# Two token units of 128 in place of one of 256 in an attention and feed-forward kernel

## The chip, the cores and the metric

The kernel runs on one core of a Trainium2 chip. The metric is the device time of one execution in microseconds (us), the median of several runs. The core has five engines that run beside each other and wait for each other through semaphores: TensorE (PE, matrix products; its weight loads are listed as PEld), VectorE (DVE), ScalarE (ACT), GpSimd (POOL) and SyncE (SP), which here issues nearly all transfers (DMA).

## The reference

Two layers run one after the other. The first is attention that keeps the 32 largest scores of each row; the second is a feed-forward layer with h - tanh(h) between its two matrices.

```python
# q, k, v: (8 batches, 8 heads, 576 tokens, 64), float32
scores = (q @ k^T) / sqrt(64)
kth    = the 32nd largest score of each row
scores = where(scores >= kth, scores, -1e9)
attn   = exp(scores - rowmax); attn = attn / (sum(attn) + 1e-9)
x      = attn @ v                  # reshaped to 4608 tokens x 512
h      = x @ w_in                  # 512 x 2048
g      = h - tanh(h)
out    = g @ w_out                 # 2048 x 512 -> 4608 x 512, float32
```

## The kernel before

**Attention in steps.** `plan()` writes a list of 144 steps. A step handles 128 rows of scores for a pair of heads (`hp`). A batch has 576 = 4 x 128 + 64 tokens: 16 steps for the four blocks of 128, and two more "rem" steps, one for every second head pair, for the last 64 tokens of the batch. So a batch has 18 steps, and half a batch nine. In each turn of the main loop, step n+1 gets its scores (`scores`, L352 on PE, copied by ACT in L360), step n is searched for its largest values on DVE (`search`, L382 to L405), step n-1 is masked and exponentiated (L438, L441, L461 on ACT and POOL), and step n-2 is divided (L487) and transposed (`turn_z`, L519). The transposed rows go through DRAM (`there`, then `spare`, L532 and L535, issued on SP), and a few steps later `values` (L583) multiplies them with v and writes tokens into a unit's `xT` or `xTr` (L603). In batch 0 the transposes are done on PE instead; in batches 1 and 2 the k and q rows are transposed on PE (L312), in the others on DVE (L319). In `scores` the pool of PSUM tiles has one buffer, so that scores of the next step cannot start before DVE has read those of the present one (L390 is its last reader).

**Feed-forward in units.** A `Unit` collects tokens: two blocks of 128 (n = 256), or one (n = 128) for the first two blocks of batch 0. The last 64 tokens of each batch are gathered over four batches into a "rest" unit of 256 with the tag `xTr`: one for batches 0 to 3, one for batches 4 to 7. The tag's pool has one buffer.

When a unit's tokens are complete, `ffn(u)` appends its items to the list `work`. Every item is eight matmul instructions; the profile shows two records for each. For a plain unit of 256 these are:

- 16 hidden items (`ffn_h`): the products with `w_in`, in column halves of 64 (`by_columns`, L627). Every second item ends with tanh and a copy on ACT (L653, L654) and a subtraction on POOL (L655), which leave g.
- 14 output items (`ffn_p`, `product`): the second matrix is applied in a form of Strassen's scheme with seven block products in place of eight. `ORDER` lists them. They need sums of blocks of g (`sum_up`, L829 on POOL), sums of blocks of `w_out` that are made once (`combine`), of which some are fetched again from DRAM for each unit (`bring`, 512 KB a time, on SP), and joins of partial results on POOL (L878).

One corner of `w_out` is changed in place by `combine("T1", ...)`: the block b12 holds b12 - b11 after it. Units of 128 (both in batch 0) use 128-column weights with 128 moving columns (L641) for their hidden items, and come before that change, so that their output items use `w_out` as it was loaded. The first unit of 256, also of batch 0, does the same with 16 output items (`plain`). The last unit of batch 7 and the rest unit of batches 4 to 7 are the tail and use `ffn_s`, which applies the seven products to `w_in` as well.

**What sets the order.** The items are dealt between the parts of the attention steps, first in, first out, by `deal`. The share of a step comes from `rate()`:

```python
have, low, high = len(work), 0.0, None
coming = sorted((t, u.items) for u, t in ready.items() if t > n)
for t, k in coming + [(NS + LAG, 0)]:
    r = have / max(t - n, 1)
    high = r if high is None else min(high, r)
    have += k
...
return max(low, high)
```

`ready` holds the step at which each unit's tokens will be complete, `u.items` the number of its items. The share is thus the largest even rate at which the list does not run dry before the next arrivals; `low` raises it where a buffer is needed again. DVE gets no item in the middle of the kernel, so the order of DVE's instructions does not depend on the shares.

Of the kernel before, what the change touches and what calls it, by code (L numbers as in the profile page):

```python
# [9 lines left out]
ALU = mybir.AluOpType  # L10
FP32 = mybir.dt.float32
# [8 lines left out]
J = 4  # L20
# [36 lines left out]
def kernel(  # L57
# [9 lines left out]
    nc = tc.nc  # L67
    P = nc.NUM_PARTITIONS
    B, H, S, D = q.shape
    DM, DFF = moe_w_in.shape  # L70
    NHP = H // 2
    JP = J * P
    R = S - JP
# [4 lines left out]
    CD = DM // P  # L78
# [5 lines left out]
    WJ = 4  # L84
    FJ = CF // WJ
# [6 lines left out]
    def pool(name, bufs, **kw):  # L92
        return ctx.enter_context(tc.tile_pool(name=name, bufs=bufs, **kw))
# [10 lines left out]
    thpool = pool("th", 4)  # L104
# [7 lines left out]
    bank = [0]  # L112

    def h_bank(k, name):
        return h_ps.tile([P, 512], FP32, tag=f"h{k}", name=name)

    def next_h(name):
        bank[0] ^= 1
        return h_bank(bank[0], name)
# [6 lines left out]
    w_out = [consts.tile([P, FJ, DM], FP32, name=f"w_out{j}") for j in range(WJ)]  # L126
# [91 lines left out]
    def half(t):  # L218
        return slice(t * D, (t + 1) * D)
# [118 lines left out]
    rest = consts.tile([P, 2, S4 + Q], FP32, name="rest")  # L338
# [230 lines left out]
    def values(n):  # L569
# [41 lines left out]
        if n in done:  # L611
            work.extend(ffn(u))
# [9 lines left out]
    cur = {}  # L622

    def by_columns(acc, lhs, rhs, start, stop):

        for t in range(2):
            nc.tensor.matmul(  # L627
                acc[half(t)], lhs[:, half(t)], rhs, start=start, stop=stop, skip_group_check=True
            )
# [45 lines left out]

    def corners(x):
        x = x.rearrange("p (m r) n -> p m r n", r=2)
        return [[x[:, :, r, c * 2 * P : (c + 1) * 2 * P] for c in range(2)] for r in range(2)]  # L680

    def keep_corner(j):

        nc.sync.dma_start(kept_B12[:, 2 * j : 2 * j + 2, :], corners(w_out[j][:])[0][1])

    def bring_corners():

        for j in range(WJ):
            nc.sync.dma_start(corners(w_out[j][:])[0][1], kept_B12[:, 2 * j : 2 * j + 2, :])

    def combine(x, j):

        (b11, b12), (b21, b22) = corners(w_out[j][:])
        k, ms = j // 2, slice(2 * (j % 2), 2 * (j % 2) + 2)
        t2 = whole["T2"][k][:, ms, :]
        if x == "T3":
            nc.gpsimd.tensor_tensor(whole["T3"][k][:, ms, :], b12, b22, ALU.subtract)
        elif x == "T1":
            nc.gpsimd.tensor_tensor(b12, b12, b11, ALU.subtract)
        elif x == "T2":  # L700
            nc.gpsimd.tensor_tensor(t2, b11, whole["T3"][k][:, ms, :], ALU.subtract)
            if k == 0:
                outgoing.append((called[0], lambda: nc.sync.dma_start(kept["T2"][:, ms, :], t2)))
        else:
            t4 = temps[j % 2] if k else whole["T4"][k][:, ms, :]
            nc.gpsimd.tensor_tensor(t4, b21, t2, ALU.subtract)
            if k:
                outgoing.append((called[0], lambda: nc.sync.dma_start(kept["T4"][:, ms, :], t4)))
# [242 lines left out]
    def ffn_small_o(u, part):  # L951

        ffn_o(u, 0, part)
        if u.combines:
            combine_next()

    def ffn_plain_o(u, item):

        ffn_o(u, item // (CF // 2), item % (CF // 2))
        if item % 2:  # L960
            combine_next()
# [13 lines left out]
    def ffn(u):  # L975

        nh = CF * u.n // (2 * P)
        full = len(u.blocks) == 2
        if u.tail:
            nh = 0  # L980
            for item in range(2 * len(ORDER)):
                yield CD * WJ, u, lambda item=item: ffn_s(u, item)
        for item in range(nh):
            f = (item + 1) * CF // nh - 1
            yield CD * (f // FJ + 1), u, lambda item=item: (ffn_full if full else ffn_h)(u, item)
        if not full:
            for part in range(CF // 2):
                yield CD * (WJ + part // 2 + 1), None, lambda part=part: ffn_small_o(u, part)
            return
        if u.plain:  # L990
            for item in range(CF):
                yield 2 * WJ * CD, None, lambda item=item: ffn_plain_o(u, item)
            return
        for item in range(2 * len(ORDER)):
            yield 2 * WJ * CD, None, lambda item=item: ffn_p(u, item)
# [3 lines left out]
    steps, done, work = [], {}, []  # L999

    def plan():
        steps.clear(), done.clear()

        def block(b, qt):
            return [(slice(0, P), out[b * S + qt * P : b * S + (qt + 1) * P, :])]

        rest = None
        for b in range(B):
            if b % 4 == 0:
                rest = Unit(  # L1010
                    [
                        [(half(i), out[(b + k + i) * S + JP : (b + k + i + 1) * S, :]) for i in range(2)]
                        for k in (0, 2)
                    ],
                    "xTr",
                )

            parts = [(0, 1), (2, 3)]
            if b == 0:
                parts[0:1] = [(0,), (1,)]  # L1020
            for a, qts in enumerate(parts):
                unit = Unit([block(b, qt) for qt in qts], "xT")
                unit.tail = b == B - 1 and a == len(parts) - 1
                if unit.tail:
                    rest.tail = True
                    unit.items = rest.items = 4 * len(ORDER)
                pe = b == 0
                unit.combines = pe and a == 1
                unit.plain = pe and a == len(parts) - 1
                if unit.plain:  # L1030
                    unit.items = 32
                for hp in range(NHP):
                    for i, qt in enumerate(qts):
                        steps.append(Step(b, hp, qt, unit, 0, i, len(qts), pe, a))
                    if hp == NHP - 1:
                        done[len(steps) - 1] = unit
                    if hp % 2 and a == (0 if b == B - 1 else len(parts) - 1):
                        steps.append(Step(b, hp - 1, J, rest, b % 4 * R, pe=pe, part=a))
                        if hp == NHP - 1 and b % 4 == 3:
                            done[len(steps) - 1] = rest  # L1040
        for g, after in zip(steps, steps[1:]):
            if after.pe and not after.rem and not g.pe:
                g.lag = 3
# [3 lines left out]

    def run(exact):
        plan()
        turned_pe[0] = not exact  # L1050
        combined[0] = 0
# [237 lines left out]
```

## Time and profile before

| | |
|---|---|
| Median of 3 runs | 1467.79 us (1467.73 to 1472.83) |
| The profiled execution | 1468.51 us |
| Its span (first to last instruction) | 1466.6 us |
| Mean granted TensorE clock | 0.970 of full speed |
| PE busy | 1366.4 us (93%), 13220 records |
| DVE busy | 1321.3 us (90%) |
| POOL busy | 1078.7 us (74%) |
| ACT busy | 1032.7 us (70%) |
| DMA | 240.83 MB, mean 164 GB/s |

The profile is of one execution. Its time is a little longer than its span, which leaves out what lies before the first and after the last instruction. "Busy" is the time in which at least one instruction of an engine runs; matmuls are pipelined and overlap, so a mean duration of one is longer than what a further one costs, and a busy PE is not PE at its peak. In a row of a group of instructions, the numbers after the bar are busy us, mean ns of one, and idle time of the engine just before them with the releasers. In a row of a wait they are us in total, how many times, and the longest.

### The profile page before, as it was taken

To read this page: it belongs to the slowest core of one execution; us is meant where nothing else is said; L and a number is where in the kernel's file an instruction comes from. 1 tells how busy PE (TensorE), PEld (TensorE's weight loads), DVE (VectorE), ACT (ScalarE), POOL (GpSimd) and SP (SyncE) were. 2 spreads that over 40 slices of the span, in tenths; PEclk is the share of its full clock that TensorE was granted. 3 is DMA by queue.
4 is the path that set the end of the run, shared out by engine and by line. 5 is a ranking of instruction groups with operands and counts; after the bars stand their busy time and mean duration, and the time that the engine had idled before them with its cause. 6 is when DMAs were issued, how large, how long until landed. Compare 5 with 4: busy or idle time off the path is not lost.

```text
span 1466.6 us, 37560 instructions
## 1 busy us (share of the span) xinstructions
PE 1366.4 (93%) x13220; PEld 864.3 (59%) x13220; DVE 1321.3 (90%) x4968; ACT 1032.7 (70%) x1916; POOL 1078.7 (74%) x1568
## 2 busy tenths in 40 slices
PE   4667899999998998999999999999999999999998
PEld 2455565345665655656656666666565666656885
DVE  7999989999999999999999999999999999886411
ACT  5776778778787867777777777777777777764421
POOL 4777688869697785969696969696978697868211
PEclk9687999999999999999999999999999999999999
DMA  9954104667767676676767767667666667643311
GB/s 282 384 184 163 51 21 106 175 161 189 202 172 194 161 179 177 166 192 158 180 181 188 170 182 172 182 164 197 167 181 172 175 163 196 156 141 109 90 53 33
DMA packets 240965, 240.83 MB, mean 164 GB/s; under 512 B 177408, under 2 KB 186112, under 8 KB 233600
## 3 DMA queue, kind: packets, MB, share of 16 engines
q1 hardware_dynamic: 238400, 238.04, 60.3%
q8 instruction: 107, 1.75, 0.5%
q14 instruction: 90, 0.74, 0.2%
q10 hardware_dynamic: 2368, 0.30, 0.2%
HBM read 152.42 MB, written 85.85 MB: 162 GB/s over the span
## 4 chain that ended last, share of the span: by engine, by line
PE 43%; DVE 37%; POOL 7%; DMA 5%; ACT 4%; issue 2%; SPq 1%; ACTq 0%; DVEq 0%; POOLq 0%
PE hps L627 13%; PE hx L627 10%; PE hy L627 8%; DVE m L402 7%; PE av L583 5%; PE scps L352 5%; DVE top L394 5%; DVE zx L519 5%; DVE rest L405 5%; DVE ab L388 3%; POOL z L441 2%; DVE top L405 2%; DVE ab L383 2%; DMA there<-zx 2%; DVE scps L382 2%
## 5 line engine op out<-in xcount | busy, mean ns | idle before, releaser
L441 POOL TENSOR_TENSOR z<-sc,z 128x576 f32<-128x576 f32 x288 | 406.3, 1433 | 64.1 <-ACT z L438 63.4
L627 PE MATMUL hps<-xT,w_in 128*64 128x256 f32 x3584 | 408.7, 383 | 3.5 <-ACT g L654 3.1
L627 PEld LDWEIGHTS hps<-xT,w_in 128*64 128x64 f32 x3584 | 251.7, 138 | 154.2 <-issue 27.6
L487 ACT ACTIVATE z<-z,rd 128x576 f32<-128x576 f32 x252 | 181.2, 767 | 93.9 <-DVE rd L480 91.0
L461 ACT ACTIVATE z<-z,nb 128x576 f32<-128x576 f32 x288 | 221.9, 776 | 8.1 <-POOL z L441 7.8
L438 ACT ACTIVATE z<-sc,tb 128x576 f32<-128x576 f32 x288 | 208.4, 776 | 22.7 <-POOL tb L419 18.1
L655 POOL TENSOR_TENSOR g<-g,th 128x512 f32<-128x512 f32 x128 | 164.2, 1283 | 63.1 <-ACT g L654 61.5
L394 DVE MAX8 top<-ab 128x8 f32<-128x144 f32 x864 | 194.5, 293 | 0.0
L360 ACT COPY sc<-scps 128x1152 f32<-128x1152 f32 x144 | 161.0, 1118 | 45.6 <-PE scps L352 44.9
L519 DVE STREAM_TRANSPOSE zx<-z 128x1152 f32<-128x1152 f32 x126 | 171.4, 1360 | 7.6 <-ACT z L487 4.9
L352 PE MATMUL scps<-kT,qT 64*64 64x288 f32 x2016 | 155.0, 423 | 23.1 <-DVE top L390 21.9
L402 DVE MAX8 m<-rest 128x8 f32<-128x168 f32 x576 | 161.1, 320 | 0.0
L402 DVE MAX8 m<-top 128x8 f32<-128x144 f32 (+1 forms) x576 | 152.2, 305 | 0.0
L627 PE MATMUL hx<-w_out,g 128*64 128x256 f32 x1024 | 123.3, 390 | 2.5 <-POOL g L655 2.4
L352 PEld LDWEIGHTS scps<-kT,qT 64*64 64x64 f32 x2016 | 67.4, 135 | 93.0 <-issue 27.5
L419 POOL TENSOR_SCALAR tb<-m 128x1 f32<-128x1 f32 x288 | 86.4, 310 | 45.4 <-DVE m L402 44.9
L627 PE MATMUL hy<-more,g 128*64 128x256 f32 x1024 | 117.8, 380 | 0.0
L388 DVE TENSOR_TENSOR ab<-scps,sc 128x576 f32<-128x576 f32 x144 | 107.5, 747 | 0.0
L653 ACT ACTIVATE th<-hps 128x512 f32<-128x512 f32 x128 | 75.1, 587 | 39.5 <-PE hps L627 35.3
L627 PEld LDWEIGHTS hx<-w_out,g 128*64 128x64 f32 x1024 | 72.4, 139 | 47.7 <-POOL g L655 5.6
L445 POOL TENSOR_SCALAR bad<-top,tb 128x3 uint8<-128x3 f32 x288 | 97.5, 347 | 0.1
L627 PEld LDWEIGHTS hy<-more,g 128*64 128x64 f32 x1024 | 72.3, 137 | 40.8 <-issue 5.4
(217 smaller groups left out, 2464.3 us busy)
## 6 DMA issues: line engine op xcount, KB each, us to landing
there<-zx SPq DMA_DIRECT2D x56, 1152.0 KB, 4.8
spare<-there SPq DMA_DIRECT2D x224, 288.0 KB, 5.4
more<-kept_T SPq DMA_DIRECT2D x31, 512.0 KB, 4.0
there<-zx SPq DMA_DIRECT2D x14, 576.0 KB, 7.0
spare<-there SPq DMA_DIRECT2D x56, 144.0 KB, 3.0
out_dram<-ot SPq DMA_DIRECT2D x31, 256.0 KB, 3.4
vb<-in_v_dram SPq DMA_DIRECT2D x48, 128.0 KB, 5.4
kin<-in_k_dram SPq DMA_DIRECT2D x82, 72.0 KB, 4.4
```

Of the source, the lines that this page charges most:

```text
L352: nc.tensor.matmul(ps[i * R : i * R + w, t, s, 0:S2], qT[g.b, hp, g.part][half(t), o : o + w], kT[g.b, hp][half(t), ks], start=True, stop= ...
L360: nc.scalar.copy(sc[:], ps[:, :, :, 0:S2])
L388: nc.vector.tensor_tensor(low[:, :, :, 0:W2], thirds(near), thirds(far), ALU.min)
L394: nc.vector.max(top[:, t, o : o + 8], low[:, t, i, :])
L402: nc.vector.max(m[:, t, m8], seen[i][t])
L438: nc.scalar.activation(zv[:, t, :], scf[:, t, :], AF.Relu, bias=tb[:, t : t + 1], scale=-BIG)
L441: nc.gpsimd.tensor_tensor(zv[:, t, :], scf[:, t, :], zv[:, t, :], ALU.subtract)
L461: nc.scalar.activation(x["zv"][:, t, :], x["zv"][:, t, :], AF.Exp, bias=x["nb"][:, t : t + 1], scale=scale, accum_out=den[:, t : t + 1],)
L487: nc.scalar.activation(x, x, AF.Copy, scale=rds[n][:, g.i, t : t + 1])
L519: nc.vector.transpose(tiles(zx, g.nq)[:, :, :, g.i, :].rearrange("p c k j -> p k c j"), z[:].rearrange("p (k c j) -> p k c j", c=NG, j=G),)
L627: nc.tensor.matmul(acc[half(t)], lhs[:, half(t)], rhs, start=start, stop=stop, skip_group_check=True)
L655: nc.gpsimd.tensor_tensor(g, g, th[:], ALU.subtract)
```

## The change

The rest unit of batches 0 to 3 becomes two units of 128 tokens: the last 64 tokens of batches 0 and 1, and those of batches 2 and 3. The rest unit of batches 4 to 7 stays as it was. Since a unit of 128 has one block, its hidden items take the form of L641, eight items for 16. Its second matrix is applied by a new function, `ffn_r`, in eight items: two accumulators (hx, hy) collect the left and the right half of the output; the first pair of items is copied out halfway because the corner b12 now holds b12 - b11, so that the product with b11 has to be added to the right half as well, which POOL does at the end. A small unit uses none of the sums of blocks and none of the blocks that `bring` fetches.

```diff
+    def ffn_r(u, item):
+
+        turn, side = item // 2, item // 2 % 2
+        r, c = turn // 2, side
+        if item == 0:
+            cur[u] = [next_h("hx"), None]
+            u.o = thpool.tile([P, DM], FP32, tag="th", name="ot")[:]
+        if item == 2:
+            cur[u][1] = h_bank(bank[0] ^ 1, "hy")
+        acc = cur[u][side][:, 0 : 2 * P]
+        for m in range(4):
+            f = 2 * (4 * (item % 2) + m) + r
+            by_columns(
+                acc,
+                u.g[0][:, f // 4, f % 4 * P : (f % 4 + 1) * P],
+                w_out[f // FJ][:, f % FJ, c * 2 * P : (c + 1) * 2 * P],
+                item in (0, 2) and m == 0,
+                item in (5, 7) and m == 3,
+            )
+        lo, hi = slice(0, 2 * P), slice(2 * P, 4 * P)
+        if item == 1:
+            nc.scalar.copy(u.o[:, hi], acc)
+        elif item == 5:
+            nc.scalar.copy(u.o[:, lo], acc)
+        elif item == 7:
+            y = thpool.tile([P, DM], FP32, tag="th", name="oy")[:]
+            nc.scalar.copy(y[:, hi], acc)
+            nc.gpsimd.tensor_tensor(u.o[:, hi], u.o[:, hi], y[:, hi], ALU.add)
+            for rows, dst in u.blocks[0]:
+                nc.sync.dma_start(dst, u.o[rows, :])
+            bank[0] ^= 1
...
     def ffn(u):
...
+        if not full and u.tag == "xTr":
+            for item in range(8):
+                yield 2 * WJ * CD, None, lambda item=item: ffn_r(u, item)
+            return
         if not full:
...
     def plan():
...
+        starts = {0: 2, 2: 4} | {x: x + 4 for x in range(4, B, 4)}
         for b in range(B):
-            if b % 4 == 0:
+            if b in starts:
+                first_b, ends = b, starts[b]
                 rest = Unit(
                     [
-                        [(half(i), out[(b + k + i) * S + JP : (b + k + i + 1) * S, :]) for i in range(2)]
-                        for k in (0, 2)
+                        [(half(i), out[(k + i) * S + JP : (k + i + 1) * S, :]) for i in range(2)]
+                        for k in range(b, ends, 2)
                     ],
                     "xTr",
                 )
...
                     if hp % 2 and a == (0 if b == B - 1 else len(parts) - 1):
-                        steps.append(Step(b, hp - 1, J, rest, b % 4 * R, pe=pe, part=a))
-                        if hp == NHP - 1 and b % 4 == 3:
+                        steps.append(Step(b, hp - 1, J, rest, (b - first_b) * R, pe=pe, part=a))
+                        if hp == NHP - 1 and b == ends - 1:
                             done[len(steps) - 1] = rest
```

## The prediction

> **What bounds the kernel now.** I read the page's 40 slices first, to see which engine is full where.
>
> ```profile
> PE   4667899999998998999999999999999999999998
> DVE  7999989999999999999999999999999999886411
> PEclk9687999999999999999999999999999999999999
> ```
>
> From slice 7 to slice 33 both TensorE (PE) and VectorE (DVE) stand at 9 tenths, so a share of busy time decides nothing. The feed-forward pieces ("items") are dealt between the attention steps, so the second view is a table of stretches of nine steps. Their borders are the starts of L382, the first DVE instruction of a step: steps 40, 49, 58, 67, 76, 85, 94, 103, 112, and 130 to 139.
>
> ```profile
> core 0: us, PE busy (x) PEld busy (x) DVE busy (x) ACT busy (x) POOL busy (x), PEclk, DMA share, GB/s
> 397.50:473.80 76.30, 73.28 (x732) 43.92 (x728) 75.99 (x301) 60.87 (x115) 62.39 (x93) 1.00 0.70 186
> 473.80:554.70 80.90, 74.47 (x754) 45.33 (x754) 79.63 (x307) 60.49 (x111) 62.41 (x93) 0.96 0.68 166
> 554.70:632.80 78.10, 75.00 (x704) 44.99 (x704) 77.44 (x303) 59.39 (x109) 61.62 (x92) 0.96 0.70 184
> 632.80:714.90 82.10, 78.58 (x766) 48.19 (x768) 79.95 (x307) 60.30 (x110) 62.83 (x93) 0.96 0.68 169
> 714.90:794.00 79.10, 76.78 (x773) 46.98 (x771) 77.20 (x303) 59.37 (x110) 62.26 (x93) 1.00 0.72 191
> 794.00:876.10 82.10, 82.10 (x830) 51.39 (x828) 79.83 (x306) 63.87 (x119) 66.10 (x96) 1.00 0.66 166
> 876.10:957.30 81.20, 81.13 (x820) 50.47 (x818) 77.56 (x302) 61.18 (x113) 65.66 (x94) 1.00 0.69 179
> 957.30:1038.30 81.00, 80.42 (x814) 49.98 (x812) 79.86 (x305) 63.54 (x118) 65.98 (x97) 1.00 0.70 169
> 1038.30:1117.00 78.70, 77.13 (x782) 47.81 (x780) 77.21 (x302) 59.77 (x109) 65.11 (x97) 1.00 0.70 186
> 1198.50:1282.80 84.30, 83.25 (x868) 52.38 (x866) 78.41 (x304) 61.06 (x117) 66.19 (x99) 1.00 0.68 182
> ```
>
> The first number after the stretch is its length; length minus DVE busy is DVE idle. In order: 0.3, 1.3, 0.7, 2.2, 1.9, 2.3, 3.6, 1.1, 1.5 and 5.9 us. So DVE sets the pace, and PE costs time only where DVE waits for it. The waits say how:
>
> ```profile
> ACT sc L360 <- PE scps L352: 44.9, 50, 5.8
> DVE scps L382 <- ACT sc L360: 35.4, 27, 6.2
> PE scps L352 <- DVE top L390: 22.1, 16, 4.9
> ```
>
> DVE starts a step when the scores (PE L352) have been copied (ACT L360); scores that stand behind too many items come late. The third line is the reverse: PE is ahead and waits until DVE has let go of the scores' PSUM.
>
> **A ledger for one stretch.** An item is eight matmul instructions, two records each; the prices are in these rows (busy over count):
>
> ```profile
> L627 PE MATMUL hps<-xT,w_in 128*64 128x256 f32 x3584 | 408.7, 383 | 3.5 <-ACT g L654 3.1 <-ACT xT L603 0.4
> L641 PE MATMUL hps<-xT,w_in 128*128 128x128 f32 x256 | 33.0, 290 | 0.0
> L829 POOL TENSOR_TENSOR g<-g 128x512 f32<-128x512 f32 x42 | 54.1, 1288 | 0.5
> L878 POOL TENSOR_TENSOR ot<-ot,oy 128x256 f32<-128x256 f32 x42 | 31.0, 739 | 19.2 <-ACT ot L921 11.3 <-ACT oy L924 7.3
> ```
>
> L627: 408.7/3584 = 0.114 us a record, so 16 records are 1.8 us an item. Counting items between score groups in the instruction order gives, for the ten stretches, 29, 28, 29, 32, 32, 35, 35, 33, 33 and 37. I take the rest of PE's work (scores, value products, changes between them) as 18.3 us a stretch: this makes 35 items 63.0 + 18.3 = 81.3 us, against 82.1 and 81.2 measured, and 37 items 84.9 against 84.3. At 33 items PE needs 77.7 us, which is less than or about DVE's 79.9 and 77.2; what stays is 1.1 and 1.5 us of DVE idle, because items come whole. So a stretch lasts about the larger of DVE busy plus 1.1 and 1.8 x items + 18.3. Batches 1 and 2 also turn their k and q on PE: 64 transposes in two batches, 12 us, so 3 us a stretch more up to step 49.
>
> **The change, part by part.**
>
> *Matmuls.* The unit of 256 had 16 hidden and 14 output items; the two of 128 have 8 + 8 each, so 32 for 30: 2 x 1.8 = 3.6 us more PE work, wherever it is placed. Output items keep their shape. Hidden ones become L641's: 33.0/256 = 0.129 us a record, but half of those ran at a clock of about 0.8; from 170 to 180 us at clock 1.00 there are 48 records in 5.47 us, 0.114 us, the price of L627. A rule of the Trainium skill speaks against this shape (TensorE: Matmul & The Clock Gate, Part 3, "What overlaps and what doesn't"): a weight load overlaps a running matmul only if its row group differs, which never holds for loads of full height. With L641's mean load of 0.210 us exposed, 256 records would cost 53.8 us more. The trace shows 32.9 us of loads inside 33.0 us of matmuls, wholly covered: I take 0.
>
> *Placement, the larger part.* Half of the rest unit's work becomes ready at the end of batch 1 instead of batch 3. The function rate() is plain arithmetic; worked through, the share at steps 39 to 47 rises from 3.34 to 3.62 items a step, and at 85 to 95 falls from 3.9 to 4.0 down to 3.72 to 3.77, with one step of 2.3. Items a stretch (40 to 120, nine stretches) go from 29, 28, 29, 32, 32, 35, 35, 33, 33 to 32, 31, 31, 31, 33, 33, 32, 33, 32: two more in all. From step 104 on the shares differ by at most 0.15, and DVE's order is the same throughout.
>
> By the ledger:
> - 94 to 102: 32 items, PE 75.9, DVE 77.6 + 1.1 = 78.7 for 81.2: -2.5.
> - 85 to 93: 33 items, 77.7; DVE 79.8 + 1.1 = 80.9 for 82.1: -1.2.
> - 67 to 75: 31 items, 74.1; DVE 80.0 + 1.1 = 81.1 for 82.1: -1.0.
> - 76 to 84: one item more, but DVE 77.2 + 1.5 = 78.7 for 79.1: -0.4. 112 to 120: -0.4.
> - 49 to 57: -0.2; 58 to 66: 78.5 for 78.1, +0.4.
> - 40 to 48: 57.6 + 18.3 + 3 = 78.9 us of PE for 76.0 of DVE, where 29 items needed 73.5. This is the one stretch that gets worse. Lower end 0: PE can run late by some 2 us before DVE notices, and steps 48 and 49 get 3 and 2 items. Upper end 4.3: three more items are 5.4 us, less the 1.1 that the clean stretches hide. I take +2.0, nearer the 2.9 of the ledger than to 0.
>
> The sum is -5.3 + 2.0 = -3.3.
>
> *Starved steps and the clock.* At the end of a part the items run out, PE idles, and its clock falls:
>
> ```profile
> 466.20:474.70 8.50, 4.58 (x44) 2.15 (x40) 8.46 (x35) 5.81 (x12) 4.44 (x8) 0.97 0.82 262
> 474.70:483.20 8.50, 6.91 (x48) 3.62 (x48) 8.46 (x35) 5.79 (x11) 4.82 (x9) 0.63 0.49 99
> 625.20:633.60 8.40, 6.94 (x70) 3.89 (x66) 8.37 (x34) 5.65 (x11) 4.68 (x9) 1.00 0.94 250
> 633.60:642.40 8.80, 7.17 (x44) 3.85 (x46) 8.77 (x35) 6.34 (x13) 5.32 (x10) 0.61 0.46 125
> ```
>
> Idle of 3.9 us at 466, and of only 1.5 us at 625, are each followed by a clock of about 0.6. The skill's rule (the same page, Part 1) is that one idle window of about 3.4 us halves the clock. In the changed kernel the starved steps get 1.3 to 1.6 items of share instead of 0.0 to 0.3, so some 2 us less idle; by the rule these falls would vanish, and with them the DVE idle just after (the 0.9 us at L382 in 473.8 to 554.7 and 0.9 + 0.4 in 632.8 to 714.9: -2.2 us). By the second pair they stay. The ledger already holds about half of this; I add 0, and keep -1.2 as the end.
>
> *POOL, ACT, DMA.* Gone for each 256: six sums of 512 columns and four of half (6 x 1.29 + 4 x 0.74), three joins (3 x 0.74) and seven ACT copies of 0.36. New: six copies and two joins. Net 11.4 us less POOL, one copy less. I cost it at 0: in these stretches POOL is busy 62 to 66 us of 76 to 82, and the waits of DVE on POOL there add up to 0.2 us. SP loses two loads of 512 KB (4.0 us each). DVE waited 0.6 and 1.3 us for DMA (zx L519 on there<-zx) in 632.8 to 714.9 and 794.0 to 876.1; between 0 and -1.9, I take 0, since which load was in the way is not shown.
>
> *New waits.* Item 4 of a small unit writes the bank that item 1's copy reads; items 2 and 3 lie between, 3.6 us over a copy of 0.36: 0; without that cover about 0.4 each. Item 1 needs the last POOL subtraction, as in the old form, once more than before: 0 to 2.5, the longest of such waits being 2.0; I take 0.3. The store of a small unit waits on SP for the POOL join, which may stand behind two masks of 1.43 us: up to 3.6 us in which `there` and `spare` transfers behind it stand still, and then DVE's next write of zx. Bounds 0 to 2 x 3.6, I take 0: values are used five steps later, and zx has a step of slack less 4.8 us for landing. The single token buffer xTr is written by the second small unit from step 53, and the first one's last hidden item is dealt by step 50: 0, with three steps as cover. In sum +0.3.
>
> Total -3.0 us. The profiled execution took 1468.51 us (span 1466.6, 1.9 outside it), 0.7 above the median 1467.79. So 1465.5 for it, and 1464.8 for the median.
>
> **Rivals.**
>
> *Overload in batch 2 (slower).* The place is 381 to 474 us. If PE can't absorb 3.62 items with the transposes, the whole 4.3 us are paid there, and the two extra items (3.6 us) are paid as well if the later idle is not about items but about whole-item steps, which stay. Between +4.3 and +7.9: 1472.1 to 1475.7, centre 1473. It decides once DVE idle in 40 to 48 exceeds the 5.3 us gained later. For it: PE was already 73.3 of 76.3 there. Against: not one DVE wait was recorded there, so there is slack of unknown size.
>
> *Idle goes altogether (faster).* DVE idle from 473.8 to 957.3 is 12.0 us; down to the floor of 0.3 a stretch that 397.5 to 473.8 shows, 10.2 us are to be had. With nothing lost in batch 2: 1457.6; with one or two, 1459. It needs the clock falls to vanish and DMA waits with them.
>
> *It does nothing that shows.* The idle moves from 794 to 957 into 397 to 474, and the sum is within 1 us: 1467.8.
>
> **Numbers.** Half a per cent is 7.3 us, about what a measurement of this kernel can tell from no change: under 1460.5 is faster, over 1475.1 slower. Mine 0.48 (1462 to 1467, with 0.03 of it below 1460.5); overload 0.20, 0.08 of it above the bound, with 0.02 for stalls not listed: slower 0.10; idle gone 0.20, 0.18 of it below the bound, with the 0.03: faster 0.21; nothing that shows 0.12. Same: the rest, 0.69. The range 1458 to 1473 leaves out about half of each outer rival.
>
> **What would show it.** DVE busy unchanged in every stretch; DVE idle 1 to 1.5 us at 85 to 93 and 94 to 102; waits of L382 on L360 new in 40 to 48, 1 to 3 us; L641 at 0.112 to 0.115 us a record; the same tail from step 130. The ledger is wrong if the idle at 85 to 102 stays above 4 us with 65 items in place of 70, or if DVE waits for anything but L360 grow.

## The result, and the profile after

| | before | changed |
|---|---|---|
| Median | 1469.26 us (1467.73 to 1472.83, 6 runs) | 1460.68 us (1459.57 to 1462.50, 6 runs) |
| The profiled execution | 1468.51 us | 1461.39 us |
| Its span | 1466.6 us | 1459.5 us |
| Mean granted TensorE clock | 0.970 | 0.980 |

The ratio of the changed kernel to the one before, run beside it, is 0.9946 with a 95% interval of 0.9935 to 0.9957: 7.9 us faster. The prediction had 3.0 us, with a range that holds the result. (1467.79 us, the median ahead of the prediction, is that of the first three of these six runs before.)

The slices of the page after. The columns of the clock row are 40 equal parts of the span:

```profile
PE   4667899989999999999999999999999999999998
DVE  7998989999999999999999999999999999896311
PEclk9787899999999999999999999999999999999999
```

TensorE (PE) is now at 9 from the tenth slice to the last but one; before, two slices there stood at 8 (the 13th and the 16th, which the prediction read as 9). The next view is the table of stretches of nine steps, cut at the starts of the same steps (40, 49, 58, and so on; the last row is 130 to 139). The first number after the stretch is its length, and length minus DVE busy is DVE idle.

```profile
core 0: us, PE busy (x) PEld busy (x) DVE busy (x) ACT busy (x) POOL busy (x), PEclk, DMA share, GB/s
400.60:479.50 78.90, 78.90 (x785) 50.82 (x782) 76.36 (x301) 61.57 (x117) 63.24 (x93) 1.00 0.71 187
479.50:559.20 79.70, 76.99 (x781) 50.13 (x782) 79.39 (x306) 62.43 (x117) 61.46 (x93) 1.00 0.63 153
559.20:636.70 77.50, 74.29 (x752) 45.83 (x748) 77.19 (x303) 58.76 (x110) 61.98 (x90) 1.00 0.73 190
636.70:716.60 79.90, 75.83 (x766) 46.83 (x764) 79.59 (x306) 59.81 (x113) 64.23 (x96) 1.00 0.68 168
716.60:794.10 77.50, 76.98 (x782) 47.71 (x780) 77.19 (x303) 58.67 (x108) 64.40 (x98) 1.00 0.73 191
794.10:876.20 82.10, 81.80 (x836) 56.24 (x834) 79.86 (x306) 61.95 (x116) 55.03 (x84) 1.00 0.69 167
876.20:954.20 78.00, 74.68 (x748) 46.08 (x746) 77.30 (x303) 59.91 (x110) 62.93 (x95) 1.00 0.72 187
954.20:1036.50 82.30, 80.88 (x834) 50.51 (x832) 79.94 (x306) 62.74 (x119) 66.79 (x102) 1.00 0.68 165
1036.50:1114.00 77.50, 74.99 (x750) 46.23 (x746) 77.19 (x303) 59.28 (x109) 63.39 (x92) 1.00 0.73 190
1195.90:1279.60 83.70, 82.82 (x859) 52.67 (x857) 78.26 (x304) 60.45 (x115) 65.12 (x99) 1.00 0.68 181
```

Three things are to be seen. DVE busy is the same as before in every stretch, to within 0.4 us. The clock column is 1.00 throughout, where three stretches had 0.96. And DVE idle from step 49 to 84 has shrunk to the floor of 0.3 us a stretch. The waits of DVE from step 49 to 102 name what went. Before, the waits for scores (L382) were 6.7 us in seven pieces, and those for transfers (L519) 1.8 us in two; after:

```profile
DVE zx L519 <- DMA there<-zx: 1.8, 2, 1.4
DVE scps L382 <- ACT sc L360: 0.4, 1, 0.4
```

So the waits for scores are gone, and those for transfers add up to what they did.

The difference of the two profiled spans, piece by piece (length after minus length before, in us):

| Steps | Difference | |
|---|---|---|
| up to 30 | +3.1 | same instruction order in both: see below |
| 40 to 48 | +2.6 | more items while PE transposes k and q of batch 2 |
| 49 to 57, 58 to 66, 67 to 75 | -1.2, -0.6, -2.2 | |
| 76 to 84, 85 to 93, 94 to 102 | -1.6, 0.0, -3.2 | |
| 103 to 138 | -0.1 | |
| 139 to the end | -3.9 | |
| sum | -7.1 | 1459.5 against 1466.6 |

Up to step 36 the two kernels issue the same instructions. In the twelve profiles of all kernels here, all the same up to there, step 31 starts between 320.1 and 324.1 us after the first instruction. The +3.1 us is thus put down to the spread of the start, and not to the change. Without it the pieces add up to -10.2 us, more than the 7.9 (6.3 to 9.6) that the ratio of all runs gives. A profile is of one execution, and no run here shows where the other 2.3 us lie. What needs a cause is -4.0 us in steps 49 to 75, -4.8 in 76 to 102, +2.6 in 40 to 48 and -3.9 in the tail. The last was in no step of the prediction.

### The profile page after: what moved, and what is told of

Same layout as the page of the kernel before. It is cut to its first block, busy times and chain, and to the rows that moved or that the text cites. A ratio compares the mean times of both kernels' runs of the same rounds, so it can differ in the third digit from the quotient of the medians.

```text
span 1459.5 us, 37602 instructions
## 1 busy us (share of the span) xinstructions
PE 1363.3 (93%) x13252; PEld 877.5 (60%) x13252; DVE 1320.7 (90%) x4968; ACT 1029.1 (71%) x1915; POOL 1066.8 (73%) x1557
## 4 chain that ended last, share of the span: by engine, by line
DVE 46%; PE 36%; DMA 6%; POOL 6%; ACT 3%; issue 2%; SPq 1%; DVEq 0%; ACTq 0%; POOLq 0%
PE hps L627 9%; PE hx L627 9%; DVE m L402 8%; PE hy L627 7%; DVE zx L519 6%; DVE top L394 6%; DVE rest L405 6%; PE av L583 4%; PE scps L352 4%; DVE ab L388 4%; DVE top L405 3%; DMA there<-zx 3%; DVE ab L383 3%; DVE scps L382 2%; POOL z L441 2%
## 5 line engine op out<-in xcount | busy, mean ns | idle before, releaser
L627 PE MATMUL hps<-xT,w_in 128*64 128x256 f32 x3584 | 405.0, 381 | 0.0
L627 PEld LDWEIGHTS hps<-xT,w_in 128*64 128x64 f32 x3584 | 251.2, 137 | 147.2 <-issue 21.4
L487 ACT ACTIVATE z<-z,rd 128x576 f32<-128x576 f32 x252 | 181.4, 767 | 134.7 <-DVE rd L480 132.9
L438 ACT ACTIVATE z<-sc,tb 128x576 f32<-128x576 f32 x288 | 208.5, 777 | 18.1 <-POOL tb L419 11.7
L519 DVE STREAM_TRANSPOSE zx<-z 128x1152 f32<-128x1152 f32 x126 | 173.5, 1377 | 7.8 <-ACT z L487 4.4
L352 PE MATMUL scps<-kT,qT 64*64 64x288 f32 x2016 | 151.3, 415 | 18.6 <-DVE top L390 15.2
L402 DVE MAX8 m<-rest 128x8 f32<-128x168 f32 x576 | 165.3, 335 | 0.0
L627 PE MATMUL hx<-w_out,g 128*64 128x256 f32 x1088 | 126.6, 381 | 6.3 <-POOL g L655 6.2
L627 PE MATMUL hy<-more,g 128*64 128x256 f32 x960 | 111.5, 381 | 0.0
L627 PEld LDWEIGHTS hx<-w_out,g 128*64 128x64 f32 x1088 | 76.2, 137 | 51.1 <-POOL g L655 8.8
L653 ACT ACTIVATE th<-hps 128x512 f32<-128x512 f32 x128 | 75.0, 586 | 34.5 <-PE hps L627 26.3
L583 PE MATMUL av<-spare,vb 128*64 128x256 f32 (+1 forms) x1056 | 94.7, 322 | 0.0
```

The source lines that it names most:

```text
L352: nc.tensor.matmul(ps[i * R : i * R + w, t, s, 0:S2], qT[g.b, hp, g.part][half(t), o : o + w], kT[g.b, hp][half(t), ks], start=True, stop= ...
L402: nc.vector.max(m[:, t, m8], seen[i][t])
L438: nc.scalar.activation(zv[:, t, :], scf[:, t, :], AF.Relu, bias=tb[:, t : t + 1], scale=-BIG)
L487: nc.scalar.activation(x, x, AF.Copy, scale=rds[n][:, g.i, t : t + 1])
L519: nc.vector.transpose(tiles(zx, g.nq)[:, :, :, g.i, :].rearrange("p c k j -> p k c j"), z[:].rearrange("p (k c j) -> p k c j", c=NG, j=G),)
L627: nc.tensor.matmul(acc[half(t)], lhs[:, half(t)], rhs, start=start, stop=stop, skip_group_check=True)
```

## The experiments

All ratios are to the kernel before, run on the same chip in the same rounds. Two kernels compared with each other are compared by these ratios, and by the stretches of their profiles, which repeat closely where the kernels do the same (steps 58 to 66 take 77.4 to 77.5 us in five profiles with the changed kernel's order there).

### The tail: one item dealt one part later or earlier

From step 133 on both kernels issue the same PE instructions, but not quite the same order on ScalarE (ACT). At each part of a step `deal` adds that part's share to a credit, and it deals items as long as the credit is above zero. Worked through, it is left with a credit of -0.036 at the last part of step 140 before the change, and of 0.056 after it, so that one hidden item more is dealt there. Before the change its tanh and copy (L653, L654) come behind the mask (L438) and the division (L487) on ACT.

`after_minus` undoes that in the changed kernel, `before_plus` does that alone in the kernel before:

```diff
+            if n == 140:
+                credit -= 0.1       # after_minus;  += 0.1 in before_plus
             share, usable, now[0] = rate(), converted[0], n
```

> The changed kernel with 0.1 taken from the dealing credit at step 140, so that the last item of that step is dealt one part later, in the order of the kernel before from there to the end. Theory A (what the tail gained is one item's place beside ACT's L438): VectorE idles 3 to 4 us at the start of step 142 again, the time is 3 to 4.5 us over the changed kernel's 1460.7, 1464 to 1465. Rival (the tail gained by chance, or by the lighter load before it): no new wait, within 1 us of 1460.7.

Measured: 1464.41 us median, ratio 0.9966 (0.9953 to 0.9979), against 0.9946 (0.9935 to 0.9957) for the changed kernel: 2.9 us lost. The intervals overlap a little; in the profiles step 139 to the end takes 182.3 us for 179.9. PE's order in time, the lines of the changed kernel first and then those of `after_minus`; in brackets the idle time before an instruction and what ended it:

```profile
1290.46 1.20 PE L352 MATMUL scps<-kT,qT 64*64 64x288 f32 x16 [1.13 <-ACT z L438]
1291.59 10.75 PE L627 MATMUL hps<-xT,w_in 128*64 128x256 f32 x96
1302.27 1.20 PE L352 MATMUL scps<-kT,qT 64*64 64x288 f32 x16
```

```profile
1290.42 9.02 PE L627 MATMUL hps<-xT,w_in 128*64 128x256 f32 x80
1301.78 1.95 PE L627 MATMUL hps<-xT,w_in 128*64 128x256 f32 x16 [2.34 <-ACT g L654]
1303.66 1.20 PE L352 MATMUL scps<-kT,qT 64*64 64x288 f32 x16
```

The sixth item needs a PSUM bank (where PE leaves its results) that ACT has not copied out, since ACT stands at L438 and L487; the scores of the next step wait behind it. That is theory A, smaller than expected: VectorE then waits 2.0 us, not 3 to 4. In the kernel before, the same gap of 2.34 us was followed by 3.4 us at a clock of 0.50, which made the same records longer:

```profile
1306.14 2.89 PE L627 MATMUL hps<-xT,w_in 128*64 128x256 f32 x16 [2.34 <-ACT g L654]
1308.96 1.89 PE L352 MATMUL scps<-kT,qT 64*64 64x288 f32 x16
```

That is 0.9 us for the item and 0.7 for the scores, 1.6 in sum, and the wait there was 3.6 us for the 2.0 of `after_minus`. So the tail's loss before the change was the item's place and, for a part, the clock once more.

> The kernel before with 0.1 added to the dealing credit at step 140: one item is dealt one part earlier, nothing else is changed. Theory A: the VectorE wait of 3.6 us at the start of step 142 goes, and the time falls by 3 to 4.5 us, ratio 0.997 to 0.998. Rival (the tail's gain needs the small units): ratio 1.000 within 0.0007.

Measured: 1465.14 us median, ratio 0.9978 (0.9968 to 0.9987), 3.2 us gained by an item's place alone (and with it the clock's fall, which its profile no longer has there). DVE idle from step 139 to 142 is 6.6 us; it is 10.6 in the kernel before and 6.5 in the changed one. So the tail's part of the gain does not need the small units. It comes from the remainder of a credit that their counts happened to leave.

### The small form without the early placement

`late_split` keeps both small units, but puts them on the list only when batch 3 is done. They share one token buffer (columns 0 and 128), and their items are taken as hidden, hidden, output, output. Its tail has the favourable order.

```diff
-                        if hp == NHP - 1 and b == ends - 1:
+                        if hp == NHP - 1 and b == ends - 1 and b != 1:
                             done[len(steps) - 1] = rest
...
         if n in done:
-            work.extend(ffn(u))
+            x, y = list(ffn(u.mate)) if u.mate is not None else [], list(ffn(u))
+            if x:
+                x, y = x[:8] + y[:8], x[8:] + y[8:]
+            work.extend(x + y)
```

> The two units of 128 kept with all their instructions, but both are put on the list only at the end of batch 3, where the unit of 256 was; both share one token buffer so that no wait is added. The tail has the changed kernel's order. Theory (placement is the cause in the middle): shares are those of the kernel before or 0.1 higher, VectorE idle from step 49 to 102 is back at 12 us or more (5.2 in the changed kernel), and only the tail's 3 to 4 us remain of the gain, less up to 2 us for two more items in the full stretches: ratio 0.997 to 1.000. Rival (the small form itself, with 11 us less POOL work and two loads less, is the cause): ratio 0.994 to 0.996, idle as in the changed kernel.

Measured: 1468.54 us median, ratio 0.9993 (0.9985 to 1.0001). DVE idle from step 49 to 102 is 12.6 us (4.2 in the changed kernel, where I had written 5.2 into the expectation). Its waits for scores in these steps, where the changed kernel has 0.4 us:

```profile
DVE scps L383 <- ACT sc L361: 7.1, 9, 1.6
```

Its clock is 0.96 again in each stretch from step 49 to 75. The proper comparison is `before_plus`, whose tail is as good: 0.9993 against 0.9978, so the small form itself costs about 2 us here (3.5 in the two profiles from step 31 on), about what two items more in full stretches should. The rival is out: placement makes the gain in the middle.

### The clock in the starved steps

`warm` is `before_plus` with junk products in the three steps whose items run out (shares below 1 at 48, 57 and 66). It keeps every item where the kernel before has it.

```diff
             deal(0.2)
+            if NEAR < n < 80 and share < 1:
+                idle = zt_ps.tile([P, 512], FP32, tag="zt", name="idle")
+                for i in range(8):
+                    nc.tensor.matmul(idle[:, 0:256], w_in[0][:, i % 4, 0:P], w_in[0][:, i % 4, 0:256], start=True, stop=True)
```

> The kernel before with the tail's order of the changed one (as in before_plus), and in steps 48, 57 and 66, whose items run out, eight more matmul instructions into a PSUM tile that nobody reads, 1.8 us, to cut the idle gaps of 4.8, 4.9 and 3.1 us. Theory (part of the gain in 473 to 715 us is that the clock no longer falls): [...]VectorE idle in steps 49, 50 and 67 to 69 (2.4 us with the floor) goes: 1.5 to 2.5 us faster than before_plus's 1465.1, ratio 0.996 to 0.997. If eight instructions are too few and gaps of 3 us remain, the clock falls at one or two places and the gain is 0.5 to 1 us. Rival (fewer items in the full steps after it, not the clock, saved that idle): the clock stays but the idle too, ratio 0.998 as before_plus.

Measured: 1464.77 us median, ratio 0.9956 (0.9941 to 0.9971), against 0.9978. The intervals overlap a little; the profiles decide. The table of stretches of `before_plus`, then that of `warm`, steps 49 to 75:

```profile
473.70:554.80 81.10, 74.41 (x754) 45.37 (x754) 79.62 (x306) 60.23 (x111) 62.36 (x93) 0.96 0.69 166
554.80:632.70 77.90, 74.78 (x704) 44.87 (x704) 77.36 (x302) 59.50 (x109) 61.65 (x92) 0.96 0.72 184
632.70:714.70 82.00, 78.46 (x766) 48.11 (x768) 80.00 (x307) 60.32 (x110) 62.85 (x93) 0.96 0.68 169
```

```profile
476.50:556.20 79.70, 75.39 (x742) 46.60 (x740) 79.39 (x307) 59.62 (x111) 62.33 (x93) 1.00 0.69 169
556.20:633.60 77.40, 75.01 (x742) 46.50 (x740) 77.09 (x302) 59.33 (x109) 61.63 (x92) 1.00 0.71 184
633.60:713.60 80.00, 78.80 (x796) 48.64 (x794) 79.69 (x307) 60.13 (x112) 62.93 (x94) 1.00 0.71 174
```

241.0 us became 237.1 with more PE work and no item moved. The changed kernel takes 79.7 + 77.5 + 79.9 = 237.1 us for the same steps. So all of its 4.0 us there are matched by the clock alone. The rest of `warm` is not all better: steps 130 to 142 take 2.5 us more than in `before_plus`, with two waits for transfers of 0.9 us each and one more fall of the clock, after a gap of 2.10 us at 1291.1 us. Why is not shown.

### What the change took off POOL and SP

`pool_back` adds eight POOL additions to the small units' hidden items, and `load_back` two loads of 512 KB, one to each unit.

```diff
             nc.gpsimd.tensor_tensor(g, g, th[:], ALU.subtract)
+            if u.tag == "xTr" and u.n == P:                      # pool_back
+                s = sums[item % 4 // 2].rearrange("p m n -> p (m n)")
+                nc.gpsimd.tensor_tensor(s, g, g, ALU.add)
...
+        if item == 2:                                            # load_back, in ffn_r
+            bring("T2")
```

> The changed kernel with one POOL addition of 512 columns (1.28 us) more behind each of the four subtractions of each small unit, written to a place that no one reads: 10.3 us of POOL work, about what the change took away (11.4). Theory (POOL is beside the path, costed at 0): VectorE idle per stretch as in the changed kernel within 0.5 us, time within 1 us of 1460.7. Rival (less POOL work is part of the gain): 2 us or more slower, with waits of PE on POOL g or of VectorE on POOL.

Measured: 1460.32 us median, ratio 0.9954 (0.9938 to 0.9969). The additions took 1.04 us each, 8.3 us in all, and DVE idle is the changed kernel's in every stretch within 0.15 us. So POOL is beside the path as far as these 8.3 us go.

> The changed kernel with one load of 512 KB put back into each small unit (the block that is there already is fetched again), two in all, as many as the change took away. Theory (costed at 0): time within 1 us of 1460.7, VectorE waits on transfers in steps 85 to 102 unchanged (1.8 us). Rival (these loads stood in the way of the `there` and `spare` transfers): 1 to 2 us slower, by waits of zx L519 on there<-zx.

Measured: 1463.03 us median, ratio 0.9966 (0.9952 to 0.9979). Its profile starts like the changed kernel's (step 31 at 324.1 us), so that the spans can be set side by side: 1461.5 against 1459.5. The waits of DVE in steps 49 to 57, where the changed kernel has none, and then in 85 to 102 (us in total, times, longest):

```profile
DVE zx L519 <- DMA there<-zx: 1.0, 1, 1.0
```

```profile
DVE zx L519 <- DMA there<-zx: 2.5, 3, 2.0
DVE scps L382 <- ACT sc L360: 0.4, 1, 0.4
```

The second was 1.8 us in two waits. On SP the load is issued at 495.1 us, just before the `there` transfer of 496.7 us, and the next write of zx waits 1.0 us for that one. So a load can stand in the way, as the rival says, and this one does. But the rival is not shown to hold for the change itself. The first load stands in step 50, where the kernel before had none of the rest unit's. The second is issued in step 89, and only 0.2 us of waits follow it up to step 102; the other 0.5 us lie in a wait of step 87, ahead of it. The loads that the change took away were issued in steps 89 and 91 before, and a wait of 1.3 us followed in step 92; neither the changed kernel nor `late_split` has it. The changed kernel has 1.8 us of such waits in steps 86 and 87 instead. What two loads less were worth to it stays open.

### Can it be had more evenly?

`rate()` does not count a unit that becomes complete in the very step, so that most arrival steps are starved and the ones after are fuller. `counted` counts it from step 45 on; `counted_late` from step 85 to 138 only, with the credit set at step 140 to give the tail the changed kernel's order; `cap` holds the share at 3.4 in steps 39 to 47; `both` does the last two.

```diff
             coming = sorted((t, u.items) for u, t in ready.items() if t > n)
+            if n >= NEAR:                                        # counted
+                have += sum(u.items for u, t in ready.items() if t == n and not u.tail)
+            if 84 < n < 139:                                     # counted_late, both
+                have += sum(u.items for u, t in ready.items() if t == n)
...
+            if n == 140:                                         # the three later ones
+                credit = -0.694
             share, usable, now[0] = rate(), converted[0], n
+            if 38 < n < 48:                                      # cap, both
+                share = min(share, 3.4)
```

> The changed kernel, with one more line in rate(): from step 45 on, a unit that becomes complete in the very step is counted among the work at hand. Shares are then 3.6 to 3.63 in every step from 39 to 138, with no starved step and none over 3.7. Theory (DVE idle follows items beyond about 3.6 a step): VectorE idle from 103 to 138 falls from about 10 us to 3, the clock's falls stay away, no loss in 40 to 48 beyond the 2.3 us of the changed kernel: 4 to 8 us faster than the changed kernel, 1453 to 1457, ratio 0.989 to 0.992. Rival (idle comes from whole items and other waits, not from the rate): within 2 us of the changed kernel.

Measured: 1464.19 us median, ratio 0.9967 (0.9956 to 0.9979): no faster than the changed kernel (its profile is 2.5 us longer), and the expectation missed. Steps 103 to 138 did as foretold (DVE idle is 4.7 us for 10.3). But steps 40 to 75, with more items than in the changed kernel, took 4.1 us more, which was not foretold. And step 139 spent five items early, so that in the tail PE had nothing to put between dependent products; from there to the end it took 7.9 us more. PE's order in time there:

```profile
1345.71 1.04 PE L627 MATMUL hy<-et,kT 128*64 128x128 f32 x16
1353.25 1.98 PE L627 MATMUL hx<-rest,ab 128*64 128x128 f32 x16 [6.49 <-ACT g L840]
```

> The changed kernel with the share held at 3.4 items from step 39 to 47, where it was 3.62; the two items that this saves are dealt later. The dealing credit is set at step 140 so that the tail keeps its order. Theory (in batch 2 PE has 73 of 76 us of work at 29 items and its own transposes): VectorE idle in steps 40 to 48 falls from 2.5 us to 0.3 to 0.8, and the rest grows by at most 0.5: 1 to 2 us faster than the changed kernel, 1458.7 to 1459.7, ratio 0.993 to 0.994. Rival (single late scores come from the order of whole items, not from the rate): idle stays at 2 us or moves to other steps, within 0.5 us of the changed kernel.

Measured: 1465.61 us median, ratio 0.9971 (0.9961 to 0.9981). The idle of 40 to 48 went (0.3 us for 2.5), and came back as 1.4 us at step 53, 1.2 at 84, 1.3 more in 85 to 93 and 1.2 more in 112 to 120. The rival was right that it moves to other steps, but not in its size: what batch 2 loses to its 32 items is less than what two fewer cost later.

> The changed kernel with arriving units counted in rate() from step 85 to 138 only, so that shares there are 3.67 to 3.78 with no step starved, and with the last arrival before the tail left as it was; the credit is set at step 140 so that the tail has the changed kernel's order. Theory (the loss in the kernel 'counted' is the tail's, whose items had been spent at step 139, and its gain of 5 us in steps 103 to 138 is real): VectorE idle in 103 to 138 is 4 to 6 us for 10.3, and the time 3 to 5 us under the changed kernel's: 1456 to 1458, ratio 0.991 to 0.992. Rival (the shorter middle is given back in the tail whatever the order there): VectorE idle falls as said, but the end stays within 1 us of 1460.7.

Measured: 1457.62 us median (1455.47 to 1459.73), ratio 0.9918 (0.9900 to 0.9935), the fastest of all, 3.1 us under the changed kernel's median (its interval just meets that one's, which starts at 0.9935). DVE idle from 103 to 138 is 6.7 us, not quite the 4 to 6 expected. In the profiles steps 85 to 138 are 3.8 us shorter and the tail 1.0 longer, with a gap of 3.59 us before the scores at 1283.6 us: the set credit did not give quite the changed kernel's tail. The stretch of steps 130 to 138:

```profile
1193.50:1272.70 79.20, 79.09 (x830) 49.68 (x828) 77.83 (x304) 60.78 (x113) 63.73 (x95) 1.00 0.73 194
```

It takes 79.2 us where the changed kernel takes 83.7.

> cap and counted_late together. If their gains lie in different steps they add up: 4 to 7 us under the changed kernel, 1454 to 1457, ratio 0.989 to 0.992. If the items that cap holds back cost in the full stretches after it what it saves, the time is that of counted_late within 0.7 us.

Measured: 1461.40 us median, ratio 0.9944 (0.9927 to 0.9960). Neither expectation held: the gains don't add up, and cap takes back 3 to 4 us of what counted_late gives.

## Why the prediction was right, and where its sum was not

*What held, and what was luck.* The mechanism of the larger part held: items placed earlier. Between groups of scores they came out as forecast in all nine stretches (32, 31, 31, 31, 33, 33, 32, 33, 32), and `late_split`, without the early placement, has none of the gain in the middle. The range held too, but the sum did not: 7.9 us are more than twice 3.0, 1460.68 us lie below the prediction's own 1462 to 1467, and it put "faster" at less than 1460.5. In the middle, the rival in which idle goes altogether was nearer: DVE idle from step 49 to 102 fell from 11.9 to 4.2 us. The falls of the clock went, as that rival asked; the waits for transfers did not. That the tail added 3.9 us was luck.

*Bound and ledger.* DVE set the pace and its busy time hardly moved. The stretches came out as: 94 to 102, -3.2 for -2.5; 76 to 84, -1.6 for -0.4; 112 to 120, -1.2 for -0.4, but 103 to 111, +1.3 for 0; 40 to 48, +2.6 for +2.0, with 1.8 us of new waits for scores, as named. 85 to 93 stayed at 82.1 us for -1.2. Two things there were not in the ledger: 1.8 us of waits for transfers, for which its 1.1 us of idle had no room, and PE, busy 81.8 us where it had 77.7. Which of them set the stretch is not shown.

*Starved steps and the clock: the term that was mis-sized.* I put 0, and -1.2 as its end; steps 49 to 75 gave -4.0 where the ledger had -0.8, and `warm` shows the whole of it without any item moved. The step that failed is "By the second pair they stay". I read two windows cut at step borders, with 1.5 and 1.6 us of idle, as two gaps. PE's order in time shows one, across the border, in the kernel before:

```profile
630.24 1.90 PE L627 MATMUL hx<-w_out,g 128*64 128x256 f32 x16
635.23 2.20 PE L352 MATMUL scps<-kT,qT 64*64 64x288 f32 x16 [3.10 <-DVE top L390]
```

and in the changed one, at the same place in the order of steps:

```profile
635.88 1.90 PE L627 MATMUL hx<-more,g 128*64 128x256 f32 x16
639.13 1.20 PE L352 MATMUL scps<-kT,qT 64*64 64x288 f32 x16 [1.36 <-DVE top L390]
```

The gaps before were 4.75, 4.85 and 3.10 us. Each brought some seven microseconds at a clock of 0.50, which began within the gap and lasted 4.7 to 6.2 us into the work after it; from step 40 to its last two microseconds the changed kernel has no gap over 1.9 us and no fall. The rule of the Trainium skill (TensorE: Matmul & The Clock Gate, Part 1) that one idle window of about 3.4 us halves the clock was the better guide, though not an exact one: 3.1 us did so too, and shorter gaps at times (see the last section). The rows of scores show the price: 16 records take 2.20 us after the gap, and 1.20 after the short one. I had also taken that the ledger held "about half of this", a half of 2.2 us; it held 0.8 of 4.0.

*The tail: missing.* "The same tail from step 130" held for PE's order, not for ACT's. I compared shares (a difference of at most 0.15) and not the credit, whose rest decides which part of a step gets an item: -3.9 us, for which `before_plus` and `after_minus` show the cause from both sides.

*Matmul form.* For the small units the group of the page after reads:

```profile
L641 PE MATMUL hps<-xTr,w_in 128*128 128x128 f32 x256 | 30.2, 277 | 0.0
L641 PEld LDWEIGHTS hps<-xTr,w_in 128*128 128x128 f32 x256 | 29.1, 192 | 2.2 <-issue 2.2
```

30.2/256 = 0.118 us a record, against 0.113 of L627 (405.0/3584): 1.3 us of PE dearer in all, for 0 predicted, and a little over the 0.112 to 0.115 that I named. The loads lie inside the matmuls, as the trace before had shown, and against the rule that I weighed and set aside.

*POOL at 0*: held (`pool_back`). *Loads at 0*: open. DVE's waits for transfers from step 49 to 102 add up to 1.8 us before and after; `load_back` shows what one load costs where none was, not what two loads less gain. *New waits at +0.3*: PE waited 3.8 us in three pieces for the last POOL subtraction from 393 to 720 us, but no wait of DVE came of it.

So the sum of 3.0 us was short by the clock (3.2 us in steps 49 to 75) and the tail (3.9). In the other stretches the errors nearly cancel: 2.7 us short in 76 to 84, 94 to 102 and 112 to 120, and 2.9 over, of which 0.6 in the transposing stretch and 1.2 in 85 to 93.

## What to carry to other kernels

Where filler work is dealt by a rate, look at the steps in which it runs out: in this kernel an idle gap of 3.1 us brought TensorE 6.2 us of work at half clock after it, and cheap junk products there showed what that is worth. Measure such a gap in the order of instructions, never in windows cut at step borders. When a change shifts how many items are dealt, compare the order on every engine to the very end, since one item before or behind a wait was worth some 3 us here, as much as the whole gain foretold for the change.

## What the runs showed of the hardware

The half clock outlasts the gap. In the kernel before, the gap from 471.5 to 476.3 us shows 0.79 in 473 to 475 and then 0.50 to 481, five microseconds into full work:

```profile
473.00:475.00 2.00, 0.00 (x0) 0.00 (x0) 1.97 (x4) 1.37 (x4) 0.66 (x4) 0.79 1.03 265
475.00:477.00 2.00, 0.71 (x8) 0.53 (x12) 2.00 (x8) 0.44 (x1) 2.00 (x2) 0.50 1.04 219
479.00:481.00 2.00, 2.00 (x12) 1.08 (x10) 2.00 (x12) 2.00 (x5) 0.06 (x1) 0.51 0.00 0
481.00:483.00 2.00, 2.00 (x22) 1.26 (x18) 1.97 (x5) 1.62 (x4) 1.15 (x5) 1.00 0.00 0
```

Shorter gaps are not decided by their length alone. 2.34 us at 1303.8 us in the kernel before and 2.10 us at 1291.1 us in `warm` were each followed by 3.4 us at half clock, but a gap of the same 2.34 us in `after_minus` and one of 2.44 us at 1042.3 us in `cap` by none.
